# Scores two blocks ahead, staged softmax and even conversion in the first 23 blocks of an attention and feed-forward kernel

## The chip, the cores and the metric

One core of a Trainium2 chip runs the whole program. The metric is the device time of one execution in microseconds (us); the median of several executions is quoted. A ratio is the mean time of one kernel's fast runs over the mean of the other's fast runs of the same rounds, so it isn't quite the ratio of the medians beside it; its bracket is a 95% interval. Ratios are to the kernel before, which ran again beside each group of experiments (medians 1627.9 to 1629.3).

Engines: PE multiplies matrices, DVE, ACT and POOL work on vectors, SP issues most transfers. Each has its own queue.

## The reference

Attention over 8 batches of 8 heads, 576 tokens of 64 elements, keeps only scores within tau of the row's maximum. Its output, 4608 x 512, goes through a feed-forward layer with a squared relu. The two weight matrices are float64, so the kernel has to convert them.

```python
scores = scale * np.matmul(q, k.transpose(0, 1, 3, 2))          # 1/8 * q k^T
thresh = np.max(scores, axis=-1, keepdims=True) - tau
scores = np.where(scores >= thresh, scores, -1000000000.0)
attn = np.exp(scores - max)                                     # cut: max of the row
attn = attn / (np.sum(attn, axis=-1, keepdims=True) + 1e-09)
x = np.matmul(attn, v)                                          # reshaped to 4608 x 512
h = np.maximum(x @ w_in, 0.0)                                   # w_in 512 x 2048
return (h * h @ w_out).astype(np.float32)                       # w_out 2048 x 512
```

## The kernel before

A *block* is 128 query rows of two heads. The first 23 blocks run while the weights arrive and are converted, one chunk of 128 x 512 a *step*. A chunk passes three stages:

```python
def convert1(m):
    a = conv.tile([P, WC], FP32, tag="a", bufs=2, name="a")
    nc.scalar.activation(out=a, in_=hi, func=AF.Abs)                  # ACT  "a"
    nc.gpsimd.tensor_scalar(out=a, in0=a, ... op0=ALU.min, op1=ALU.max)  # POOL clamp
    r = conv.tile([P, WC], I32, tag="r", bufs=2, name="r")            # two buffers
    nc.scalar.activation(out=r, in_=lo, func=AF.Copy, scale=2.0**-29) # ACT  "r"
def convert2(m):      # two DVE operations on the raw words (shift, merge)
def convert3(m):      # POOL: w_in or w_out = raw + r; frees r
    nc.gpsimd.tensor_tensor(out=chunks[m][0], in0=lo, in1=r, op=ALU.add)

def weights_step():   # (cut)
    m = at_step["n"]; at_step["n"] = m + 1
    convert3(m - 4)
    convert1(m - 2)   # its r is the buffer that convert3(m - 4) reads
    convert2(m - 3)
    if m < len(chunks): fetch(m)
```

With two buffers, the new `r` of a step may be written only after the POOL addition of the same step. In the old softmax a step stands between the exponentials (ACT) and the masks (DVE), so POOL gets that addition ahead of the block's normalisation:

```python
def begin(n, between=lambda: None):
    i, t = slots[n]
    job = softmax(i, t, scores(i, t))
    next(job)            # maxima, threshold, exponentials
    between()            # weights_step()
    next(job, None)      # masks with row sums, +1e-9, reciprocal, POOL normalisation
```

Of the kernel before, what the change touches and what calls it, by code (L numbers as in the profile page):

```python
# [13 lines left out]
ALU = mybir.AluOpType  # L14
# [5 lines left out]
def kernel(  # L20
# [27 lines left out]
    nc = tc.nc  # L48
    B, H, S, D = q.shape
    P = 128  # L50
    DM, FF = moe_w_in.shape
# [114 lines left out]
    def minus(e, out, x, y):  # L166
        e.tensor_tensor(out=out, in0=x, in1=y, op=ALU.subtract)  # L167

    def plus(e, out, x, y):
        e.tensor_tensor(out=out, in0=x, in1=y, op=ALU.add)  # L170

    def combine_in(n):

        e = nc.gpsimd
        first, second = ts(n, WC), ds(HF + n * WC, WC)
        a11, a12 = w_in[:, 0:2, first], w_in[:, 2:4, first]
        a21, a22 = w_in[:, 0:2, second], w_in[:, 2:4, second]
        s1, s2, s4 = (s_in[:, m, :, first] for m in range(3))
        yield plus(e, s1, a21, a22)
        yield minus(e, a21, a11, a21)  # L180
        yield minus(e, s2, s1, a11)
        yield minus(e, s4, a12, s2)

    def combine_out(k):

        first, second = ds(k, 4), ds(KF + k, 4)
        b11, b12 = w_out[:, first, 0:HD], w_out[:, first, HD:DM]
        b21, b22 = w_out[:, second, 0:HD], w_out[:, second, HD:DM]
        t1, t2, t4 = (t_out[0][:, m, first, :] for m in range(3))
        minus(nc.vector, t1, b12, b11)  # L190
        yield minus(nc.gpsimd, b12, b22, b12)
        minus(nc.vector, t2, b22, t1)
        yield minus(nc.gpsimd, t4, b21, t2)

    w_out_t = moe_w_out.rearrange("(f p) o -> p f o", p=P)
    chunks = [
# [8 lines left out]
    def weights_step():  # L205

        m = at_step["n"]
        at_step["n"] = m + 1
        convert3(m - 4)
        convert1(m - 2)  # L210
        convert2(m - 3)
        if m < len(chunks):
            fetch(m)
        if m - 4 in (n_in // 2 - 1, n_in - 1):
            sums_due.append(combine_in((m - 4) // (n_in // 2)))
        if m == len(chunks) + 3:
            early.close()
            late = ctx.enter_context(tc.tile_pool(name="late", bufs=1, side="right"))
            t_out.append(late.tile([P, 3, KF, HD], FP32, name="t_out"))
            sums_due.extend(combine_out(k) for k in range(0, KF, 4))  # L220

    def sums_step():
        while sums_due:
# [55 lines left out]
    def turn(i):  # L279
        qn, kn, rn = loaded.pop(i)  # L280
        qT = sb.tile([P, S], FP32, tag="qT", bufs=2, name="qT")
        kT = sb.tile([P, S], FP32, tag="kT", bufs=2, name="kT")
        _, t0, t1 = visits[i]
        for nat, to, u0, u1 in ((qn, qT, t0, min(t1, FULL)), (kn, kT, 0, FULL)):
            pt = bank([P, FULL, P], "pqk")
            for t in range(u0, u1):
                nc.tensor.transpose(pt[:, t, :], nat[:, t, :], ident[:, :])  # L287
            flat, to = pt[:, u0:u1, :].rearrange("p t m -> p (t m)"), to[:, u0 * P : u1 * P]
            if nat is qn:
                nc.scalar.activation(out=to, in_=flat, func=AF.Identity, scale=qscale[:, :])  # L290
            else:
                nc.vector.tensor_copy(out=to, in_=flat)
        pt = bank([P, P], "pqkr")
        nc.tensor.transpose(pt[:, :], rn[:, :], ident[:, :])
        nc.scalar.activation(out=qT[:, MAIN:S], in_=pt[:, 0:REST], func=AF.Identity, scale=qscale[:, :])
        nc.scalar.copy(kT[:, MAIN:S], pt[:, REST:P])
        if i < NP:
            for j in range(2):
                rows = ds(j * D, D)
                nc.gpsimd.tensor_copy(out=kdiag[i % 2][rows, ds(j * REST, REST)], in_=kT[rows, MAIN:S])  # L300
        turned[i] = (qT, kT)
# [31 lines left out]
    def softmax(i, t, sc):  # L333

        nj = 2 if t < FULL else 1
        at = (0, (psum["n"] - 1) * BANK - REST)[0:nj]
        sm = sb.tile([P, 2], FP32, tag="sm", bufs=3, name="sm")
        nmx = sb.tile([P, 2], FP32, tag="nmx", bufs=3, name="nmx")
        for j in range(nj):
            nc.vector.tensor_reduce(  # L340
                out=nmx[:, j : j + 1], in_=sc[:, ds(at[j], S)], axis=AXIS.X, op=ALU.max, negate=True
            )

        thr = sb.tile([P, 2], FP32, tag="thr", bufs=3, name="thr")
        nc.vector.tensor_scalar(
            out=thr[:, 0:nj], in0=nmx[:, 0:nj], scalar1=-1.0, scalar2=tau_p[:, :], op0=ALU.mult, op1=ALU.subtract
        )
        w = sb.tile([P, 2 * S], FP32, tag="w", bufs=2, name="w")
        for j in range(nj):
            nc.scalar.activation(  # L350
                out=w[:, ts(j, S)], in_=sc[:, ds(at[j], S)], func=AF.Exp, bias=nmx[:, j : j + 1], scale=1.0
            )
        yield
        for j in range(nj):
            nc.vector.scalar_tensor_tensor(  # L355
                out=w[:, ts(j, S)], in0=sc[:, ds(at[j], S)], scalar=thr[:, j : j + 1], in1=w[:, ts(j, S)],
                op0=ALU.is_ge, op1=ALU.mult, accum_out=sm[:, j : j + 1],
            )
        nc.vector.tensor_scalar(out=sm[:, 0:nj], in0=sm[:, 0:nj], scalar1=1e-9, scalar2=None, op0=ALU.add)
        nc.vector.reciprocal(out=sm[:, 0:nj], in_=sm[:, 0:nj])  # L360
        if t == FULL:

            normalize(w[:, S : S + REST], w[:, MAIN:S], sm[:, 0:1])
        for j in range(nj):
            normalize(w[:, ts(j, S)], w[:, ts(j, S)], sm[:, j : j + 1])
        weights[i, t] = w
# [257 lines left out]
    slots = [(i, t) for i, (_, t0, t1) in enumerate(visits) for t in range(t0, t1)]  # L624
    n_first, n_batch = NP * HALF, NP * NB

    def begin(n, between=lambda: None):
        i, t = slots[n]
        job = softmax(i, t, scores(i, t))
        next(job)  # L630
        between()
        next(job, None)

    def values_after(n):

# [9 lines left out]
            feed_forward_until(b * S + min(t1 * P, S))  # L645
        return True

    def turns(n):

        i, t = slots[n]  # L650
        return i + 1 < len(visits) and t == max(visits[i][2] - 2, visits[i][1])

    def slot(n, steps):


        def weights_due(k):
            if k < steps:
                if at_step["n"] < N_STEPS:
                    weights_step()
                sums_step()  # L660

        if turns(n):
            turn(slots[n][0] + 1)
        if n + 1 < len(slots):
            begin(n + 1, lambda: weights_due(0))
        with_values = values_after(n - 1)
        if turns(n) and slots[n][0] + 2 < len(visits):
            load(slots[n][0] + 2)
        i, t = slots[n - 1]
        if with_values and part_of(t)[1] == visits[i][2] and i + 2 < len(visits):  # L670
            load_v(i + 2)
        transposes(*slots[n])
        for k in range(1, steps):
            weights_due(k)
        return with_values

    ET = mybir.EngineType
    with ExitStack() as stack, tc.manual_schedule(engines={ET.PE, ET.DVE, ET.Activation, ET.Pool}):
        open_psum(stack, 3, 2, 2)
        load(0)  # L680
        for _ in range(2):
            weights_step()
        load(1)
        load_v(0)
        load_v(1)
        turn(0)
        begin(0)
        for n in range(n_first - 1):
            slot(n, 1)
    with ExitStack() as stack:  # L690
        g_pool = stack.enter_context(tc.tile_pool(name="g", bufs=1))
        open_psum(stack, 4, 1, 4)
        late = 0.0

        n_early = n_first - 1 + (N_STEPS + 4 - n_first) // 2
        for n in range(n_first - 1, len(slots)):
            early_on = n < n_early
            with tc.manual_schedule(engines={ET.PE, ET.DVE, ET.Activation, ET.Pool} if early_on else {ET.PE}):
                with_values = slot(n, 2 if early_on else 1)
                if n < n_first:  # L700
                    continue


                if early_on:
                    per_slot = 14 * U_IN / (n_early - n_first)
                elif n < n_batch:
                    per_slot = (asked["us"] + PIECE) / (2 * n_batch - n)
                elif n < 2 * n_batch:
                    per_slot = asked["us"] / (2 * n_batch - n)
                else:  # L710
                    per_slot = asked["us"] / (n_batch - n % n_batch)

                late = min(run(per_slot * (0.7 if with_values else 1.2) + late), 0.0)
        with tc.manual_schedule(engines={ET.PE}):
            values_after(len(slots) - 1)
            run(float("inf"))


def as_float(bits):
# [33 lines left out]
```

## Time and profile before

| kernel before | |
|---|---|
| time, median of 3 (range) | 1628.0 us (1627.81 to 1628.55) |
| profiled span, mean granted PE clock | 1626.5 us, 0.971 |
| the cut: transposes of block 23 done | 231.6 us |
| after the cut | 1394.9 us, PE busy 97% |
| ACT waiting for POOL before r, up to the cut | 44.9 us |

The cut splits the span into a stretch that the change rewrites, bound by a chain of waits, and one bound by PE. The lines stand in the prediction below. A line of the waits reads: engine, its instruction, "<-" what ended the wait, then the sum in us, how often, and the longest.

### The profile page before, as it was taken

Reading aid. Unit: us, or ns where it says so; the run is one execution under the profiler, and the core shown is the slowest. Engines: PE = TensorE matmul, PEld = TensorE weight load, DVE = VectorE, ACT = ScalarE, POOL = GpSimd, SP = SyncE. Lnnn points to the kernel's source line nnn. Section 1 sums busy time; section 2 is a strip of 40 time slices with the busy share of each in tenths; the row PEclk is TensorE's granted clock in tenths of the full one; section 3 lists DMA queues with packets and bytes.
Section 4 is the critical chain, followed back from the end, with each engine's and each line's share of the span. In section 5 each row is a group of like instructions: output and inputs, shape, how many; then the busy total and the mean of one; then the engine's idle time right before and its main releaser. Section 6 shows DMA issues by size and latency. Waiting matters only on the chain.

```text
span 1626.5 us, 25919 instructions
## 1 busy us (share of the span) xinstructions
PE 1515.6 (93%) x10084; PEld 1216.1 (75%) x10084; DVE 867.0 (53%) x1792; ACT 585.7 (36%) x1273; POOL 592.1 (36%) x630
## 2 busy tenths in 40 slices
PE   5676789999999999999999999999999999999998
PEld 2344567778787778778788887878777787878987
DVE  4678974645555564646444455555646464553222
ACT  3545633434343333433333243333433333431100
POOL 2488662332424232334141424232423333233131
PEclk8877889999999999999999999999999999999999
DMA  4334401111010101010101010101011101000000
GB/s 126 109 108 131 128 22 35 23 29 30 23 36 14 31 23 35 23 36 16 35 8 30 21 36 10 34 23 35 23 36 23 35 16 29 15 1 14 14 14 14
DMA packets 107914, 58.69 MB, mean 36 GB/s; under 512 B 89873, under 2 KB 99089, under 8 KB 107793
## 3 DMA queue, kind: packets, MB, share of 16 engines
q1 hardware_dynamic: 107792, 57.04, 12.9%
q8 instruction: 80, 1.31, 0.3%
q14 instruction: 42, 0.34, 0.1%
HBM read 47.58 MB, written 9.44 MB: 35 GB/s over the span
## 4 chain that ended last, share of the span: by engine, by line
PE 77%; DVE 12%; ACT 6%; POOL 3%; issue 2%; SPq 0%; DMA 0%; ACTq 0%; DVEq 0%; POOLq 0%
PE ph L482 27%; PE po L556 25%; PE sc L326 11%; PE pwT L397 6%; DVE nmx L340 5%; ACT w L350 4%; PE pv L428 3%; PE pqk L287 2%; PE pwR L386 2%; DVE s L170 1%; DVE w L355 1%; ACT x L436 1%; PE pv L423 1%; DVE g L491 1%; POOL w L369 1%
## 5 line engine op out<-in xcount | busy, mean ns | idle before, releaser
L369 POOL TENSOR_SCALAR w<-w,sm 128x576 f32<-128x576 f32 (+1 forms) x320 | 237.4, 752 | 643.9 <-DVE sm L360 638.4
L340 DVE TENSOR_REDUCE nmx<-sc 128x1 f32<-128x576 f32 x288 | 206.1, 752 | 206.7 <-PE sc L326 188.9
L355 DVE SCALAR_TENSOR_TENSOR w<-sc,thr,w 128x576 f32<-128x576 f32 x288 | 225.0, 815 | 132.7 <-ACT w L350 130.2
L350 ACT ACTIVATE w<-sc,nmx 128x576 f32<-128x576 f32 x288 | 199.8, 741 | 259.0 <-DVE nmx L340 258.9
L556 PE MATMUL po<-w_out,g 128*128 128x256 f32 x1152 | 261.5, 382 | 11.2 <-ACT x L436 6.1
L556 PEld LDWEIGHTS po<-w_out,g 128*128 128x128 f32 x1152 | 216.1, 191 | 41.0 <-ACT x L436 7.3
L326 PE MATMUL sc<-kT,qT 64*128 64x64 f32 (+3 forms) x1248 | 215.6, 461 | 24.5 <-DVE w L355 24.4
L482 PE MATMUL ph<-x,w_in 128*128 128x128 f32 x1728 | 209.5, 278 | 2.1 <-ACT x L436 2.1
L326 PEld LDWEIGHTS sc<-kT,qT 64*128 64x128 f32 (+1 forms) x1248 | 105.5, 181 | 137.1 <-issue 124.6
L482 PEld LDWEIGHTS ph<-x,w_in 128*128 128x128 f32 x1728 | 203.2, 195 | 3.2 <-ACT x L436 2.3
L397 PE MATMUL pwT<-ident,w 128*128 128x128 f32 x1024 | 146.3, 281 | 44.2 <-ACT x L436 25.7
L397 PEld LDWEIGHTS pwT<-ident,w 128*128 128x128 f32 x1024 | 117.1, 143 | 56.8 <-ACT x L436 37.1
L398 ACT COPY wT<-pwT 128x512 f32<-128x512 f32 x256 | 145.2, 594 | 24.6 <-PE pwT L397 20.8
L482 PE MATMUL ph<-xt,s_in 128*128 128x128 f32 x1152 | 142.4, 278 | 4.3 <-POOL s_in L167 3.3
L428 PE MATMUL pv<-wT,va 128*64 128x320 f32 (+1 forms) x1024 | 141.8, 420 | 0.0
L482 PEld LDWEIGHTS ph<-xt,s_in 128*128 128x128 f32 x1152 | 136.0, 194 | 6.2 <-POOL s_in L167 4.9
L170 DVE TENSOR_TENSOR u<-ph,u 128x512 f32<-128x512 f32 x108 | 74.6, 690 | 112.4 <-PE ph L482 84.2
L556 PE MATMUL po<-t_out,g 128*128 128x256 f32 x576 | 132.2, 379 | 0.0
L428 PEld LDWEIGHTS pv<-wT,va 128*64 128x64 f32 x1024 | 69.4, 140 | 66.5 <-issue 29.9
L556 PEld LDWEIGHTS po<-t_out,g 128*128 128x128 f32 x576 | 107.7, 190 | 13.5
L493 POOL TENSOR_TENSOR g<-p 128x512 f32<-128x512 f32 x36 | 37.8, 1049 | 156.4 <-ACT p L510 156.4
L482 PE MATMUL ph<-x,s_in 128*128 128x128 f32 x576 | 71.9, 279 | 0.0
(79 smaller groups left out, 1623.6 us busy)
## 6 DMA issues: line engine op xcount, KB each, us to landing
kn<-in_k_dram SPq DMA_DIRECT2D x72, 128.0 KB, 3.1
va<-in_v_dram SPq DMA_DIRECT2D x36, 256.0 KB, 2.8
out_dram<-o SPq DMA_DIRECT2D x36, 256.0 KB, 2.0
raw<-in_moe_w_in_dram SPq DMA_DIRECT2D x16, 512.0 KB, 4.0
raw<-in_moe_w_out_dram SPq DMA_DIRECT2D x16, 512.0 KB, 3.8
qn<-in_q_dram SPq DMA_DIRECT2D x56, 128.0 KB, 2.4
rn<-in_q_dram SPq DMA_DIRECT2D x36, 32.0 KB, 2.4
rn<-in_k_dram SPq DMA_DIRECT2D x36, 32.0 KB, 2.7
```

Of the source, the lines that this page charges most:

```text
L170: e.tensor_tensor(out=out, in0=x, in1=y, op=ALU.add)
L326: nc.tensor.matmul(to, qT[rows, ds(t * P, m)], kT[rows, ds(k0, n)], start=True, stop=True)
L340: nc.vector.tensor_reduce(out=nmx[:, j : j + 1], in_=sc[:, ds(at[j], S)], axis=AXIS.X, op=ALU.max, negate=True)
L350: nc.scalar.activation(out=w[:, ts(j, S)], in_=sc[:, ds(at[j], S)], func=AF.Exp, bias=nmx[:, j : j + 1], scale=1.0)
L355: nc.vector.scalar_tensor_tensor(out=w[:, ts(j, S)], in0=sc[:, ds(at[j], S)], scalar=thr[:, j : j + 1], in1=w[:, ts(j, S)], op0=ALU.is_ge, ...
L369: nc.gpsimd.tensor_scalar(out=out, in0=w, scalar1=r, scalar2=1.0, op0=ALU.mult, op1=ALU.mult)
L397: nc.tensor.transpose(pt[:, c, :], w[:, ds(j * (S + REST) + c * P, P)], ident[:, :])
L398: nc.scalar.copy(wT[:, j, :, at], pt[:, :, :])
L428: nc.tensor.matmul(pv[rows, :], va[:, j, c, :], wT[:, j, c, 0:n], start=False, stop=(c == FULL - 1), skip_group_check=True,)
L482: nc.tensor.matmul(to[:, j, :], a, b, start=(not more and j == 0 and c == 0), stop=(c == 1), skip_group_check=True,)
L493: e.tensor_tensor(out=to, in0=c[:, :, :], in1=c[:, :, :], op=ALU.mult)
L556: nc.tensor.matmul(to[:, :], a[:, f, :], b[:, f, :], start=(not more and f == 0), stop=(f == KF - 1), skip_group_check=True,)
```

## The change

Its intent: take scores and maxima out of the chain of a block by computing them two blocks ahead in two three-bank buffers, and let the stages of two succeeding softmaxes interleave. With it come even conversion (two steps on even blocks, one on odd), two tiny operations moved from DVE to POOL, the first feed-forward products grouped by bank, and the output weights' sums regrouped. The core of the diff:

```diff
 def softmax(i, t, sc):
+        early = psum["n"] == 3
+        small = nc.gpsimd if early else nc.vector
 ...
+            if early and j == 0:
+                yield                      # after the first maximum
-        nc.vector.tensor_scalar(           # threshold
+        small.tensor_scalar(
 ...
+        if early:
+            yield                          # before the exponentials
 ...
-        nc.vector.tensor_scalar(out=sm ... scalar1=1e-9 ...)
+        small.tensor_scalar(out=sm ... scalar1=1e-9 ...)
+        if early:
+            yield
         nc.vector.reciprocal(...)          # then the POOL normalisation
 ...
+    def early_slot(n, last, steps, ff_steps):
+        if n < last:
+            ahead(n + 2)                   # scores, two blocks ahead
+        stage(n + 1)                       # exponentials, masks, 1e-9
+        stage(n + 2)                       # first maximum
+        stage(n + 1)                       # reciprocal, POOL normalisation
+        if n < last:
+            turn_until(n + 3)
+        stage(n + 2)                       # second maximum, threshold
+        if steps:
+            weights_step()
+        for _ in range(ff_steps):
+            run(0.1)
+        values_and_load(n)
+        transposes(*slots[n])
+        for _ in range(steps - 1):
+            weights_step()
+        sums_step()
 ...
+        FF_STEPS = {11: 3, 12: 4, 17: 3, 18: 4}
+            steps = min(2 - n % 2, N_STEPS - at_step["n"])
```

The normalisation is now issued before `weights_step()`, so POOL's addition, and with it ACT's `r`, stands behind it.

More of the change, by code (lines that the diff above doesn't have):

```diff
@@ L179, in combine_in, with combine_out @@
         yield plus(e, s1, a21, a22)
+        yield minus(e, s2, s1, a11)
         yield minus(e, a21, a11, a21)
-        yield minus(e, s2, s1, a11)
         yield minus(e, s4, a12, s2)
-    def combine_out(k):
-        first, second = ds(k, 4), ds(KF + k, 4)
-        b11, b12 = w_out[:, first, 0:HD], w_out[:, first, HD:DM]
-        b21, b22 = w_out[:, second, 0:HD], w_out[:, second, HD:DM]
-        t1, t2, t4 = (t_out[0][:, m, first, :] for m in range(3))
-        minus(nc.vector, t1, b12, b11)
-        yield minus(nc.gpsimd, b12, b22, b12)
-        minus(nc.vector, t2, b22, t1)
-        yield minus(nc.gpsimd, t4, b21, t2)
+    def combine_out():
+        for what in range(2):
+            for k in range(0, KF, 4):
+                first, second = ds(k, 4), ds(KF + k, 4)
+                b11, b12 = w_out[:, first, 0:HD], w_out[:, first, HD:DM]
+                b21, b22 = w_out[:, second, 0:HD], w_out[:, second, HD:DM]
+                t1, t2, t4 = (t_out[0][:, m, first, :] for m in range(3))
+                if what == 0:
+                    minus(nc.vector, t1, b12, b11)
+                    yield minus(nc.gpsimd, b12, b22, b12)
+                else:
+                    minus(nc.vector, t2, b22, t1)
+                    yield minus(nc.gpsimd, t4, b21, t2)
     w_out_t = moe_w_out.rearrange("(f p) o -> p f o", p=P)
@@ L219, in weights_step @@
             t_out.append(late.tile([P, 3, KF, HD], FP32, name="t_out"))
-            sums_due.extend(combine_out(k) for k in range(0, KF, 4))
+            sums_due.append(combine_out())
     def sums_step():
@@ L296, in turn @@
         nc.scalar.copy(kT[:, MAIN:S], pt[:, REST:P])
-        if i < NP:
+        if psum["n"] == 3:
             for j in range(2):
@@ L352, in softmax @@
             )
-        yield
         for j in range(nj):
@@ L358, in softmax @@
             )
-        nc.vector.tensor_scalar(out=sm[:, 0:nj], in0=sm[:, 0:nj], scalar1=1e-9, scalar2=None, op0=ALU.add)
+        small.tensor_scalar(out=sm[:, 0:nj], in0=sm[:, 0:nj], scalar1=1e-9, scalar2=None, op0=ALU.add)
+        if early:
+            yield
         nc.vector.reciprocal(out=sm[:, 0:nj], in_=sm[:, 0:nj])
@@ L625, with begin @@
     n_first, n_batch = NP * HALF, NP * NB
-    def begin(n, between=lambda: None):
+    def begin(n):
         i, t = slots[n]
-        job = softmax(i, t, scores(i, t))
-        next(job)
-        between()
-        next(job, None)
+        for _ in softmax(i, t, scores(i, t)):
+            pass
     def values_after(n):
@@ L646, in values_after, with turn_until, values_and_load @@
         return True
-    def turns(n):
-        i, t = slots[n]
-        return i + 1 < len(visits) and t == max(visits[i][2] - 2, visits[i][1])
-    def slot(n, steps):
-        def weights_due(k):
-            if k < steps:
-                if at_step["n"] < N_STEPS:
-                    weights_step()
-                sums_step()
-        if turns(n):
-            turn(slots[n][0] + 1)
-        if n + 1 < len(slots):
-            begin(n + 1, lambda: weights_due(0))
+    first_slot = [n for n, (i, t) in enumerate(slots) if t == visits[i][1]]
+    turned_to = {"n": 0}
+    def turn_until(n):
+        i = turned_to["n"]
+        if i == len(visits) or first_slot[i] > n:
+            return
+        turn(i)
+        turned_to["n"] = i + 1
+        if i + 1 < len(visits):
+            load(i + 1)
+    def values_and_load(n):
         with_values = values_after(n - 1)
-        if turns(n) and slots[n][0] + 2 < len(visits):
-            load(slots[n][0] + 2)
         i, t = slots[n - 1]
@@ L671, in slot, with stage, ahead @@
             load_v(i + 2)
+        return with_values
+    def slot(n):
+        turn_until(n + 2)
+        if n + 1 < len(slots):
+            begin(n + 1)
+        with_values = values_and_load(n)
         transposes(*slots[n])
-        for k in range(1, steps):
-            weights_due(k)
-        return with_values
+        return with_values
+    jobs = {}
+    def stage(n):
+        if n in jobs:
+            next(jobs[n], None)
+    def ahead(n):
+        i, t = slots[n]
+        jobs[n] = softmax(i, t, scores(i, t))
+    def early_slot(n, last, steps, ff_steps):
[16 more added lines that the diff above has]
+        sums_step()
     ET = mybir.EngineType
-    with ExitStack() as stack, tc.manual_schedule(engines={ET.PE, ET.DVE, ET.Activation, ET.Pool}):
+    ALL = {ET.PE, ET.DVE, ET.Activation, ET.Pool}
+    g_pool = ctx.enter_context(tc.tile_pool(name="g", bufs=1))
+    with ExitStack() as stack, tc.manual_schedule(engines=ALL):
         open_psum(stack, 3, 2, 2)
@@ L682 @@
             weights_step()
-        load(1)
         load_v(0)
+        turn_until(0)
+        ahead(0)
+        stage(0), stage(0)
         load_v(1)
-        turn(0)
-        begin(0)
-        for n in range(n_first - 1):
-            slot(n, 1)
-    with ExitStack() as stack:
-        g_pool = stack.enter_context(tc.tile_pool(name="g", bufs=1))
+        ahead(1)
+        stage(0), stage(1), stage(0), stage(1)
+        turn_until(2)
+        FF_STEPS = {11: 3, 12: 4, 17: 3, 18: 4}
+        n = 0
+        while at_step["n"] < N_STEPS:
+            steps = min(2 - n % 2, N_STEPS - at_step["n"])
+            early_slot(n, 10**6, steps, FF_STEPS.get(n, 0))
+            n += 1
+        early_slot(n, n, 0, 0)
+        while sums_due:
+            sums_step()
+        n_early = n + 1
+    with ExitStack() as stack, tc.manual_schedule(engines={ET.PE}):
         open_psum(stack, 4, 1, 4)
         late = 0.0
-        n_early = n_first - 1 + (N_STEPS + 4 - n_first) // 2
-        for n in range(n_first - 1, len(slots)):
-            early_on = n < n_early
-            with tc.manual_schedule(engines={ET.PE, ET.DVE, ET.Activation, ET.Pool} if early_on else {ET.PE}):
-                with_values = slot(n, 2 if early_on else 1)
-                if n < n_first:
-                    continue
-                if early_on:
-                    per_slot = 14 * U_IN / (n_early - n_first)
-                elif n < n_batch:
-                    per_slot = (asked["us"] + PIECE) / (2 * n_batch - n)
-                elif n < 2 * n_batch:
-                    per_slot = asked["us"] / (2 * n_batch - n)
-                else:
-                    per_slot = asked["us"] / (n_batch - n % n_batch)
-                late = min(run(per_slot * (0.7 if with_values else 1.2) + late), 0.0)
-        with tc.manual_schedule(engines={ET.PE}):
-            values_after(len(slots) - 1)
-            run(float("inf"))
+        for n in range(n_early, len(slots)):
+            with_values = slot(n)
+            if n < 2 * n_batch:
+                per_slot = asked["us"] / (2 * n_batch - n)
+            else:
+                per_slot = asked["us"] / (n_batch - n % n_batch)
+            late = min(run(per_slot * (0.7 if with_values else 1.2) + late), 0.0)
+        values_after(len(slots) - 1)
+        run(float("inf"))
 def as_float(bits):
```

## The prediction

> **What bounds the kernel now.** I read the page's slices first, then three stretches side by side, then the waits of the first stretch, then that stretch in order of time. The slices say where idle TensorE time is left:
>
> ```profile
> PE   5676789999999999999999999999999999999998
> PEclk8877889999999999999999999999999999999999
> ```
>
> One slice is 40.7 us. Only the first six have PE below 90% and a clock below full. The cut at 232 us is where both kernels stand at the same place of their PE program: the transposes of block 23 are done, the 14 product groups of the first feed-forward piece are done, and the first output product comes next (the PE order of both builds shows this, and the trace has the first "po" at 231.6 us).
>
> ```profile
> core 0: us, PE busy (x) PEld busy (x) DVE busy (x) ACT busy (x) POOL busy (x), PEclk, DMA share, GB/s
> 0.00:75.00 75.00, 46.37 (x200) 25.51 (x200) 38.34 (x91) 32.57 (x69) 25.27 (x45) 0.82 0.44 120
> 75.00:232.00 157.00, 112.12 (x648) 79.80 (x647) 131.53 (x210) 79.24 (x169) 124.89 (x111) 0.80 0.37 104
> 232.00:1626.00 1394.00, 1357.11 (x9239) 1110.78 (x9238) 697.09 (x1492) 473.94 (x1037) 441.94 (x474) 1.00 0.09 24
> ```
>
> After 232 us PE is busy 1357 of 1394 us (97%) at full clock: that part is bound by PE, its work is the same in the changed kernel, and I carry it over unchanged. Before it no engine is full (DVE 170 of 232 us, POOL 150, ACT 112), so a chain of waits bounds it: 24 blocks in 231.6 us. Who waits there:
>
> ```profile
> ACT w L350 <- DVE nmx L340: 47.6, 16, 8.6
> ...
> ACT r L144 <- POOL w_out L164: 24.7, 9, 5.7
> POOL w L369 <- DVE sm L360: 21.9, 18, 6.7
> ACT r L144 <- POOL w_in L164: 20.2, 6, 5.6
> ```
>
> The exponential waits for the maximum of scores just computed, and the conversion's second activation (r) waits 45 us in all for POOL's last conversion step. The reader should keep that second wait in mind. One early block in order of time:
>
> ```profile
> 42.49 0.49 PE L330 MATMUL sc<-kdiag,qT 128*128 128x128 f32 x2
> ...
> 43.02 1.42 DVE L340 TENSOR_REDUCE nmx<-sc 128x1 f32<-128x576 f32 x2 [2.02 <-PE sc L330]
> ...
> 44.53 1.37 ACT L350 ACTIVATE w<-sc,nmx 128x576 f32<-128x576 f32 x2 [2.30 <-DVE nmx L340]
> ...
> 45.94 0.82 DVE L355 SCALAR_TENSOR_TENSOR w<-sc,thr,w 128x576 f32<-128x576 f32 x1 [0.18 <-ACT w L350]
> 46.35 0.66 ACT L144 ACTIVATE r<-raw 128x512 int32<-128x512 uint32 x1
> ...
> 46.91 0.25 ACT L388 COPY wR<-pwR 128x128 f32<-128x128 f32 x1
> ...
> 47.21 1.12 PE L397 MATMUL pwT<-ident,w 128*128 128x128 f32 x4 [3.69 <-ACT wR L388]
> ...
> 47.54 0.17 DVE L359 TENSOR_SCALAR sm<-sm 128x2 f32<-128x2 f32 x1
> 47.74 0.17 DVE L360 RECIPROCAL sm<-sm 128x2 f32<-128x2 f32 x1
> ...
> 48.07 1.47 POOL L369 TENSOR_SCALAR w<-w,sm 128x576 f32<-128x576 f32 x2 [0.92 <-DVE sm L360]
> 48.37 0.58 ACT L398 COPY wT<-pwT 128x512 f32<-128x512 f32 x1 [0.72 <-PE pwT L397]
> ```
>
> Read it as a loop: scores, maxima 1.42, exponentials 1.37, the activations a and r (1.1 from start to start), copy of the remainder, the last four transposes 1.12, and only then the next scores, because PE runs in order. Scores of succeeding blocks start at 41.4, 50.3, 58.2, 67.0 and 75.1 us: 8.4 us a block with one conversion each. From 76 to 231 us, with two conversions a block, the single four-bank buffer and the feed-forward, it is about 9.7.
>
> **What the Trainium skill says.** "PSUM — Partial Sum Buffer", Engine vs sequencer instructions: ScalarE, VectorE and GpSimdE queues are strict FIFO. The trace agrees: the copy at 46.91 starts only after r at 46.35, though its transpose had been done since 43. My argument rests on this. "SBUF — State Buffer", Who interferes with whom: DVE in a two-port mode, or with two SBUF inputs, and GpSimd exclude each other for a whole instruction. The trace agrees: the DVE conversion shift takes 0.42 us alone but 906 ns on average over the first 232 us. "TensorE: Matmul & The Clock Gate", What's actually happening: idle windows of about 3.4 us halve PE's clock; the first four transposes of that block take 0.60 us, the last four, after 3.7 us of waiting, 1.12.
>
> **The change, part by part.**
>
> *Removed from the loop:* the scores and the wait for the fresh maximum. Scores now come two blocks ahead in two three-bank buffers, and the maxima of block n+2 are taken while block n+1 is finished. Alone, this takes some 4 us (scores 2.5, maxima 1.4) off the loop.
>
> *Moved:* the threshold and the 1e-9 addition go from DVE to POOL. DVE loses at most 10.0+8.2 us over the stretch, much of it lock waiting; POOL gains two tiny operations a block, about 0.2 us each (an estimate from the 0.23 us of the small kdiag copies).
>
> *Even conversion:* two steps on even blocks and one on odd, from the start, 34 in 23 blocks; the same total work.
>
> *Added:* here the build's order and its semaphore waits decide. In a block POOL now has: 1e-9, two normalisations (n+1), the threshold (n+2), and only then the conversion's last step. ACT has: exponentials (n+1), a, r, the copies of block n, on even blocks another a and r, exponentials (n+2). r uses one of two buffers, and waits for the POOL conversion step of the same turn. So this closed loop is in the program, one block long: exponentials (n+1), DVE masks, DVE maximum (n+2), reciprocal, POOL normalisations, threshold, conversion, ACT r, copies, exponentials (n+2). With durations of the block above:
>
> - exponentials and hand-over 1.41; masks 1.60 (45.94 to 47.54); one maximum 0.71; reciprocal and hand-over 0.33: 4.05
> - normalisations 1.47, plus 0.25 which I choose for the DVE conversion now colliding with the second one; threshold 0.25: 1.97
> - POOL conversion 1.29, hand-over 0.04, r to the copy 0.56: 1.89
> - copy to transposes 0.30, transposes and hand-over 1.16 (cold clock), copy 0.48: 1.94
>
> Sum 9.85 us on an odd block. An even block adds a and r, 1.12: 11.0. A turn adds the two kdiag copies, 0.5, and a block with values 0.2.
>
> Blocks 1 to 20 have an r: ten at 9.85 and ten at 11.0, turns 7 x 0.5, values 8 x 0.2, less about 2 for each of four half-size blocks: 205 us. *Feed-forward:* with two banks, grouped products put PE work into that loop in blocks 11, 12, 17 and 18. In 11 and 17 the value product waits for the bank which the relu frees: copy 0.7, second product group 2.2, relu 0.7, values 3.1, some 6.7 us. In 12 and 18 the five DVE additions stand before the transposes' banks, some 3.4. Together 20. The start up to the reciprocal of block 2 I walk through as 27 us, and blocks 21 to 23, without r, take 5 and 3.
>
> 27 + 205 + 20 + 8 = 260 us against 231.6: about 29 longer. The regrouped output sums leave POOL two 2.35 us operations just after the cut; I charge 2 us. 1628 + 31 gives 1659, and I put 1660.
>
> **Rivals.**
>
> *The overlap works.* If POOL's late conversion step did not stop ACT, the bound would be the fullest engine: POOL's 150 us plus 10, or DVE's 170 less what the moves free. With start-up that is 175 to 190 us for the stretch, 40 to 55 us less, a time near 1580. For it speaks that no engine is full before and that scores, maxima and exponentials wait so long. Against it: the wait of r on POOL costs 45 us already in the old order, where that step stands ahead of the normalisation, and the build shows it behind. Even with no cold clock (0.5 less), no collision (0.25) and half the feed-forward cost, 20 blocks bring the cut to about 235, not below 230.
>
> *Idle moves but little changes.* If normalisations overlap better and PE stays warm, the loop is near 9.1 and 10.2, the cut near 240, the time 1635 to 1645.
>
> *More is lost.* A longer ACT wait leaves PE idle over 3 us a block, so its clock drops; at half clock the grouped products, 2 us each, take 3 to 4, and collisions of DVE with POOL's 2.35 us sums fall into the loop. Then the cut is at 275 to 285, and the time 1670 to 1685.
>
> **Range and chances.** The closed loop is in the program, so I give gain over 2% (below 1596) only 6%, for the case that I misread an order. The centre is almost on the upper edge of the 2% band (1660.6): 0.46 within and 0.48 slower. The 8-in-10 range, 1636 to 1685, spans the last two rivals.
>
> **What would show it.** In the changed profile: the first output product near 260 us and the rest still about 1395 us; r waiting for POOL's w_in and w_out steps rising from 45 us to 70 or more, with 3 to 4 us each time; the wait of exponentials for maxima nearly gone; the early clock no higher than 0.8; alternating block periods of about 10 and 11 us, and blocks 11 and 17 near 17. I am wrong if the blocks come every 7 us, or if r hardly waits: then the POOL order did not bind. I am also wrong if the stretch after the cut changes by over 10 us.

## The result, and the profile after

The changed kernel takes **1679.82 us** (1676.79 to 1680.05, 4 runs) against 1627.9 (1627.66 to 1628.55). The ratio is 1.0314 [1.0296, 1.0332]: 3.1% slower. That is inside the predicted range, 20 us above the predicted time. Its profiled span is 1678.1 us.

The slices of the page of the changed kernel, 42 us each:

```profile
PE   5557477999999999999999999999999999999999
PEclk8777777999999999999999999999999999999999
```

At the start, seven slices instead of six are now below 90%, and they are emptier. The three stretches, with the cut at 276 us:

```profile
core 0: us, PE busy (x) PEld busy (x) DVE busy (x) ACT busy (x) POOL busy (x), PEclk, DMA share, GB/s
0.00:75.00 75.00, 40.44 (x166) 21.85 (x167) 36.51 (x72) 31.39 (x64) 31.06 (x59) 0.83 0.45 121
75.00:276.00 201.00, 126.78 (x657) 81.67 (x658) 105.61 (x179) 82.13 (x174) 129.23 (x156) 0.76 0.29 81
276.00:1678.00 1402.00, 1362.36 (x9240) 1112.70 (x9240) 707.05 (x1492) 473.81 (x1036) 454.26 (x479) 0.99 0.09 24
```

More exactly the cut lies at 275.8 us, where it was 231.6: 44.2 us of the 51.6 us more of span. The other 7.4 come after it (1402.3 against 1394.9). No engine is full: DVE is busy for 142 of the first 276 us, POOL for 160. What ACT waits for up to the cut:

```profile
ACT r L144 <- POOL w_in L164: 58.8, 11, 6.5
ACT r L144 <- POOL w_out L164: 48.3, 9, 7.0
...
ACT w L360 <- DVE nmx L346: 7.2, 3, 3.8
```

The exponentials' wait for maxima has fallen from 47.6 to 7.2 us, as the change intends. The wait of `r` for POOL has risen from 44.9 to 107.1 us, 20 times. One even block in order of time (start, duration, then engine, line and operation; the bracket is idle time before it and what ended it):

```profile
57.57 1.38 ACT L360 ACTIVATE w<-sc,nmx 128x576 f32<-128x576 f32 x2
...
59.44 0.82 DVE L364 SCALAR_TENSOR_TENSOR w<-sc,thr,w 128x576 f32<-128x576 f32 x1 [6.18 <-PE sc L330]
...
61.59 0.16 DVE L371 RECIPROCAL sm<-sm 128x2 f32<-128x2 f32 x1
...
62.27 2.14 POOL L380 TENSOR_SCALAR w<-w,sm 128x576 f32<-128x576 f32 x2 [0.96 <-DVE sm L371]
...
64.41 0.31 POOL L353 TENSOR_SCALAR thr<-nmx,tau_p 128x2 f32<-128x2 f32 x1
64.68 1.28 POOL L164 TENSOR_TENSOR w_in<-raw,r 128x512 int32<-128x512 int32 x1
...
66.00 0.67 ACT L144 ACTIVATE r<-raw 128x512 int32<-128x512 uint32 x1 [6.51 <-POOL w_in L164]
...
66.82 0.27 ACT L399 COPY wR<-pwR 128x128 f32<-128x128 f32 x1
...
66.98 1.82 PE L408 MATMUL pwT<-ident,w 128*128 128x128 f32 x8 [4.29 <-ACT x L447]
...
69.88 0.66 ACT L144 ACTIVATE r<-raw 128x512 int32<-128x512 uint32 x1
...
70.43 1.37 ACT L360 ACTIVATE w<-sc,nmx 128x576 f32<-128x576 f32 x2
```

Follow the starts: exponentials, masks, reciprocal, normalisation, threshold, POOL's addition, `r`, the copy, the transposes, a second `r`, and the next exponentials 12.86 us after the first. (Three of its parts are longer than in other blocks; the sum below sets two of those beside it.) ACT stands still 6.51 us before `r`, and PE 4.29 us behind ACT, because the copies that free PE's banks stand behind `r`. The scores two blocks ahead are long ready; nobody can use them.

After the cut, the start of the tail shows where part of the 7.4 us goes:

```profile
277.01 1.21 DVE L167 TENSOR_TENSOR t_out<-w_out 128x1024 f32<-128x1024 f32 x1
277.26 3.88 POOL L380 TENSOR_SCALAR w<-w,sm 128x64 f32<-128x64 f32 x2 [0.36 <-PE sc L330]
...
281.19 0.47 PE L397 MATMUL pwR<-ident,w 128*128 128x128 f32 x1 [4.06 <-POOL w L380]
```

The regrouped weight sums run on DVE beside POOL's normalisation of block 24 (one operation of 128 x 64 and one of 128 x 576), which takes 3.88 us where it took 1.15 in the kernel before, and PE waits 4.06 us for it. Only then, at 282.3 us, comes the first output product.

### The profile page after: what moved, and what is told of

Read it like the earlier page. It is cut to its first block, busy times and chain, and to the rows that moved or that the text cites. A ratio compares the mean times of both kernels' runs of the same rounds, so it can differ in the third digit from the quotient of the medians.

```text
span 1678.1 us, 25857 instructions
## 1 busy us (share of the span) xinstructions
PE 1529.6 (91%) x10060; PEld 1216.2 (72%) x10060; DVE 849.2 (51%) x1742; ACT 587.3 (35%) x1273; POOL 614.5 (37%) x692
## 3 DMA queue, kind: packets, MB, share of 16 engines
q8 instruction: 80, 1.31, 0.3%
## 4 chain that ended last, share of the span: by engine, by line
PE 75%; DVE 10%; ACT 7%; POOL 5%; issue 2%; DMA 0%; SPq 0%; ACTq 0%; DVEq 0%; POOLq 0%
PE ph L493 27%; PE po L567 24%; PE sc L330 10%; PE pwT L408 6%; DVE nmx L346 4%; ACT w L360 4%; PE pv L439 3%; DVE w L364 2%; POOL w L380 2%; PE pwR L397 2%; PE pqk L291 1%; DVE s L170 1%; ACT x L447 1%; PE pv L434 1%; DVE g L167 1%
## 5 line engine op out<-in xcount | busy, mean ns | idle before, releaser
L567 PE MATMUL po<-w_out,g 128*128 128x256 f32 x1152 | 265.9, 385 | 7.7 <-DVE g L167 7.1
L408 PE MATMUL pwT<-ident,w 128*128 128x128 f32 x1024 | 152.5, 287 | 80.7 <-ACT x L447 40.3
L330 PE MATMUL sc<-kT,qT 64*128 64x512 f32 (+3 forms) x1200 | 214.4, 474 | 11.8 <-DVE w L364 8.7
L330 PEld LDWEIGHTS sc<-kT,qT 64*128 64x128 f32 (+1 forms) x1200 | 99.1, 181 | 120.4 <-issue 98.5
L439 PEld LDWEIGHTS pv<-wT,va 128*64 128x64 f32 x1024 | 69.3, 139 | 65.9 <-issue 27.8
L493 PE MATMUL ph<-xt,w_in 128*128 128x128 f32 x576 | 70.4, 275 | 1.4 <-DVE u L170 1.4
```

Of the source, the lines that this page charges most:

```text
L330: nc.tensor.matmul(to, qT[rows, ds(t * P, m)], kT[rows, ds(k0, n)], start=True, stop=True)
L408: nc.tensor.transpose(pt[:, c, :], w[:, ds(j * (S + REST) + c * P, P)], ident[:, :])
L439: nc.tensor.matmul(pv[rows, :], va[:, j, c, :], wT[:, j, c, 0:n], start=False, stop=(c == FULL - 1), skip_group_check=True,)
L493: nc.tensor.matmul(to[:, j, :], a, b, start=(not more and j == 0 and c == 0), stop=(c == 1), skip_group_check=True,)
L567: nc.tensor.matmul(to[:, :], a[:, f, :], b[:, f, :], start=(not more and f == 0), stop=(f == KF - 1), skip_group_check=True,)
```

## The experiments

**Theory 1:** the loss comes from `r` waiting for a POOL addition that now stands behind the normalisation. **Rivals:** the small operations on POOL; the grouped feed-forward products; the even conversion; or a full or colliding pair of POOL and DVE, whatever the order. All kernels gave correct results. The cut is read as in the profiles above, and "after cut" is the profiled span less the cut.

| run | time, median | ratio to before | cut | after cut |
|---|---|---|---|---|
| before | 1627.9 | 1 | 231.6 | 1394.9 |
| after | 1679.8 | 1.0314 | 275.8 | 1402.3 |
| r3 | 1633.2 | 1.0027 | 231.2 | 1398.9 |
| conv_first | 1635.1 | 1.0042 | 231.6 | 1400.5 |
| before_r3 | 1627.0 | 0.9994 | 229.1 | 1396.1 |
| small_dve | 1675.8 | 1.0292 | 274.4 | 1400.6 |
| ff_late | 1679.5 | 1.0304 | 252.8 | 1425.4 |
| r3_ff_late | 1630.4 | 1.0004 | 201.7 | 1426.8 |
| r3_clamp | 1641.2 | 1.0071 | 234.5 | 1403.0 |
| r3_clamp_xt | 1638.1 | 1.0050 | 237.1 | 1399.1 |
| r3_free | 1626.0 | 0.9980 | 223.7 | 1402.7 |
| before_even | 1621.7 | 0.9960 | 223.7 | 1395.6 |
| r3_free_dve | 1616.4 | 0.9919 | 215.6 | 1397.7 |
| before_late3 | 1686.9 | 1.0353 | 290.9 | 1393.9 |

### r3: a third buffer for r in the changed kernel

```diff
-        r = conv.tile([P, WC], I32, tag="r", bufs=2, name="r")
+        r = conv.tile([P, WC], I32, tag="r", bufs=3, name="r")
```

> The changed kernel with three r buffers in place of two, nothing else. Theory 1 (r waits for POOL's last conversion step behind the normalisations, and holds up ACT's copies and the next exponentials): r's wait for POOL falls from 107 us to under 50, the loop shrinks to about 8 us a block (on even blocks the second r still waits for the first step), the cut after the transposes of block 23 moves from 276 us to about 215, the time is 1610 to 1630. Theory 2 (a full engine or the DVE-POOL handing to and fro of threshold and 1e-9 bounds the block): the cut stays above 260 us, the time 1665 to 1682.

Measured: 1633.16 us (1628.62 to 1635.01), ratio 1.0027 [1.0007, 1.0047]. The cut moves by 44.6 us, and the time by 46.7 of the 52 us lost. Nothing is removed from any engine. The waits of `r` for POOL up to 232 us in this run:

```profile
ACT r L144 <- POOL w_out L164: 5.0, 5, 1.5
...
ACT r L144 <- POOL w_in L164: 4.4, 5, 1.9
```

107.1 us have become 9.4 (the two sums). The third buffer lets `r` wait for the addition of the step before instead of that of its own step. The direction is theory 1's, but I had hoped for more: the time lies 3 us above my range and the cut 16 us after my 215.

### conv_first: the order instead of the buffer

```diff
         if n < last:
             ahead(n + 2)
+        convert3(at_step["n"] - 4)
         stage(n + 1)
```

> The changed kernel with two r buffers, but the first conversion step of a block is issued on POOL ahead of the 1e-9 addition and the normalisations. Theory 1: same cause removed by order in place of a buffer, so r's first wait goes; on even blocks the second r still waits behind the normalisations, a loop of about 8 us; cut at 210 to 230 us, time 1610 to 1635. Theory 2: POOL's work is the same, cut above 260, time 1665 to 1682.

Measured: 1635.09 us, ratio 1.0042 [1.0027, 1.0056]. With two buffers still, but with POOL's addition ahead of the normalisation, the cut comes at 231.6. A different edit to the same wait has the same result, so it isn't memory or an accident of placement that made r3 faster. Here `r` still waits 36.0 us for POOL up to the cut (19.4 and 16.6), 26.6 us more than in r3, and yet the cut is the same within 0.5 us: the sum of a wait is not its price.

### before_r3: the third buffer in the kernel before

The edit of r3, in the kernel before.

> The kernel before with three r buffers: the control. Theory 1: its early blocks are bound by scores, maxima, exponentials, so the first 75 us stay; between 75 and 232 us r waits some, so 0 to 12 us less: 1616 to 1628. If a third r buffer alone gave as much here as in the changed kernel (over 40 us), the r wait would not be what the change brought in.

Measured: 1627.02 us, ratio 0.9994 [0.9979, 1.0009], cut 2.5 us earlier. The control shows that a third buffer is worth nothing clear of noise by itself. It isn't that `r` had nothing to wait for. Up to the cut of this run:

```profile
ACT w L350 <- DVE nmx L340: 76.7, 25, 10.8
...
ACT r L144 <- POOL w_in L164: 1.0, 1, 1.0
```

With 0.4 us for w_out, `r` waits 1.4 us instead of 44.9, but the exponentials wait 76.7 us for their maxima instead of 47.6. In the old order the wait of `r` cost next to nothing, because the wait for the maxima took its place.

### small_dve: threshold and 1e-9 back on DVE

```diff
-        small = nc.gpsimd if early else nc.vector
+        small = nc.vector
```

> The changed kernel with threshold and 1e-9 back on DVE. Theory 1: the threshold leaves POOL's queue ahead of the conversion step (0.3 us a block less in the loop), the 1e-9 comes back behind DVE work: within 10 us, 1668 to 1688. Theory 2 (the handing to and fro over POOL bounds the block): 30 us or more faster, under 1650.

Measured: 1675.79 us, ratio 1.0292 [1.0277, 1.0308]; this interval overlaps that of the changed kernel. The cut moves by 1.4 us. `r` still waits 100.2 us for POOL (55.8 and 44.4). The tiny operations aren't the cause.

### ff_late and r3_ff_late: no feed-forward product before the cut

```diff
-        FF_STEPS = {11: 3, 12: 4, 17: 3, 18: 4}
+        FF_STEPS = {}
```

> The changed kernel with no feed-forward products among the first 23 blocks: the 14 product groups of the first piece go to the blocks after. My prediction's term: they put 20 us into the early loop, so the cut (end of the transposes of block 23) moves from 276 to 250 to 258 us, and 14 groups of 1.8 us (25 us of PE) come after it: time within 8 us of the changed kernel, 1672 to 1686. If the cut moves by under 10 us the term was too large; by over 30 too small, and the time drops below 1672.

> The same on the version with three r buffers. There blocks 11, 12, 17, 18 took some 36 us more than their neighbours, so the cut should move from 231 to about 195 and the time from 1633 to 1618 to 1626. If the products were hidden beside other waits, the time rises by up to 25 us to 1658.

Measured: ff_late 1679.47 us (1.0304), cut 23.0 us earlier; r3_ff_late 1630.43 us (1.0004 [0.9989, 1.0019]), cut 29.5 us earlier than in r3. In both the time after the cut grows by as much (23.1 and 27.9 us). The time of r3_ff_late and its cut are 4 and 7 us above what I expected. So the grouped products cost the early stretch about what my sum said, 23.0 us for 20 in the changed kernel, but the same PE work costs that much wherever it lies; grouping them early neither loses nor gains.

### r3_clamp and r3_clamp_xt: half of the conversion moved

r3 with, in each block,

```diff
         stage(n + 1)
+        if steps:
+            convert1(at_step["n"] - 2)    # a, clamp, r ahead of the first maximum of n + 2
         stage(n + 2)
```

and in r3_clamp_xt also the four sums of the first feed-forward input after block 9 instead of at block 11 (`if n == 9: combine_x(0)`).

> Three r buffers, and a and r with POOL's clamp issued ahead of the normalisations. In the r3 trace DVE's second conversion of even blocks waits 23 us in all for that clamp, so even blocks are near 9.3 us and odd ones 6.5. If this is what is left of the loop, even blocks fall to about 7.5, the cut from 231 to about 212, the time to 1608 to 1620. If POOL itself is full by then, no change: 1628 to 1638.

> The same with the sums of the first piece's x made on POOL after block 9, in place of block 11, where PE waited 5.4 us for them: 4 to 8 us less than r3_clamp, if the products' place in the loop is what costs there; no change if those sums only move the wait.

Measured: r3_clamp 1641.22 us (1.0071 [1.0056, 1.0086]), a clear miss: I had expected a gain over r3 and it lost 8 us. r3_clamp_xt, at 1638.07 us, is 3 us better than r3_clamp, where I had expected 4 to 8; its cut is even later (237.1 against 234.5), so what it gains lies after the cut. In r3_clamp the starts of the remainder's transposes still came 10.5 and 11.2 us apart on even blocks and 7.0 on odd ones. The second `r` of an even block still waited for a POOL addition that stood behind the normalisation (1.71 us for the one at 57.15): I had moved one wait out of the loop and left its twin in. That can explain why nothing was gained; why 8 us were lost stays open.

### r3_free: both moved

```diff
+        if steps:
+            convert3(at_step["n"] - 4)
         stage(n + 1)
+        if steps:
+            convert1(at_step["n"] - 2)
         stage(n + 2)
```

> The changed kernel with three r buffers, and in each block the POOL conversion step moved ahead of the first softmax stage and the pair a, r of the next chunk with it between the stages, so that no activation of the conversion and no DVE shift stands behind a normalisation of the same block. Theory A (in the three-buffer version the even blocks are set by conversion steps that still queue behind the normalisation and the threshold; the earlier attempt moved only half of them): even blocks fall from about 9.3 to about 7.5 us, the cut (transposes of block 23) comes at 205 to 215 us instead of 231, and the time is 1605 to 1622. Theory B (with the r wait gone the stretch is bound by POOL and DVE work that excludes each other and by the landing of the raw chunks, whatever the order): the cut stays at 226 to 238 us and the time at 1628 to 1642.

Measured: 1625.97 us (1623.26 to 1628.18), ratio 0.9980 [0.9963, 0.9996]; cut 223.7 us. Each theory was half right. The two-head blocks of the first visits now come every 7.0 to 7.2 us, even and odd alike (remainder transposes at 43.81, 50.87, 58.08 and 65.05 us), which is theory A; the kernel before takes 8.4. But the cut fell between the two predictions, because the next visits are bound by something else. The next block has its transposes at 67.99 and the one after at 83.09 us. POOL in between, with the DVE operation that waits for it:

```profile
70.41 2.36 POOL L170 TENSOR_TENSOR s_in<-w_in 128x1024 f32<-128x1024 f32 x1
...
72.72 1.29 POOL L164 TENSOR_TENSOR w_in<-raw,r 128x512 int32<-128x512 int32 x1
...
74.11 0.22 POOL L368 TENSOR_SCALAR sm<-sm 128x2 f32<-128x2 f32 x1
74.36 0.17 DVE L371 RECIPROCAL sm<-sm 128x2 f32<-128x2 f32 x1 [2.19 <-POOL sm L368]
...
75.11 2.16 POOL L380 TENSOR_SCALAR w<-w,sm 128x576 f32<-128x576 f32 x2
```

The 0.22 us addition of 1e-9 stands behind a weight sum of 2.36 and a conversion step of 1.29 us. DVE idles 2.19 us for it, and the normalisation and the next exponentials follow late. With `r` freed, the placement of the small operations should begin to matter.

### r3_free_dve: and the small operations back on DVE

r3_free with the edit of small_dve.

> The version with three r buffers and the reordered conversion, with the threshold and the 1e-9 addition back on DVE. In that version's trace DVE waits 16.8 us for the 1e-9 addition on POOL, which stands behind the 2.35 us weight sums and the last conversion step. Theory (with r freed, POOL sets the pace of the three-block visits): cut 213 to 220 us instead of 223.7, time 1615 to 1623. Rival (DVE, which would take on the two small operations and their lock waits, sets it): cut 223 or later, time 1625 to 1632.

Measured: 1616.36 us (1615.04 to 1617.83), ratio 0.9919 [0.9899, 0.9938]; cut 215.6 us. Both numbers lie in the range of the theory, outside that of the rival. The same edit brought 4 us in the changed kernel, with overlapping intervals, and 9.6 us here. This version beats both kernels: 3.8% below the changed one and 0.8% below the kernel before (medians), which is clear of the noise but small. Its slices:

```profile
PE   6775889999999999999999999999999999999998
...
PEclk9879899999999999999999999999999999999999
```

### before_even: the even conversion alone, in the kernel before

```diff
-            slot(n, 1)
+            slot(n, 2 - n % 2)
 ...
-        n_early = n_first - 1 + (N_STEPS + 4 - n_first) // 2
+        n_early = 23
 ...
-                with_values = slot(n, 2 if early_on else 1)
+                with_values = slot(n, (2 - n % 2) if early_on else 1)
```

> The kernel before with one part of the change alone: two conversion steps on every even block and one on every odd one from the start, in place of one a block at first and two a block later. Theory A (the loss of the change comes from r standing behind the normalisation, which this order of the softmax does not have): the time stays within 1620 to 1640 and the r wait for POOL under 60 us. Rival (the even conversion itself costs the early blocks, because it puts second activations into blocks that had one): cut at 245 us or later, time 1643 to 1660.

Measured: 1621.69 us, ratio 0.9960 [0.9945, 0.9975]; cut 223.7 us, `r` waits 25.3 us. So this part of the change is a small gain, and not the cause of the loss.

### before_late3: the suspected order put into the kernel before

```diff
         next(job)
-        between()
         next(job, None)
+        between()
```

> The mirror: the kernel before with one thing of the change put into it, the whole conversion step placed after the normalisation instead of between the exponentials and the masks. If r waiting behind the normalisation is the cause, the loop scores, maxima, exponentials, masks, normalisation, last conversion step, r, copy, transposes, scores closes at about 10.3 us in the blocks of one step instead of 8.4, and some 1.5 us more in the blocks of two: the cut goes from 231.6 to 255 to 275, the waits of r for POOL from 45 us to over 80, the time to 1650 to 1675. Rival (the loss belongs to the scores-ahead order, and the place of the conversion does not matter by itself): cut below 240, time 1622 to 1638.

Measured: 1686.89 us (1686.47 to 1690.04), ratio 1.0353 [1.0334, 1.0372]; cut 290.9 us. No scores ahead, no even conversion, no small operations on POOL, and yet the loss is as large as the whole change's, indeed larger than I expected. One block of this run:

```profile
51.63 1.37 ACT L350 ACTIVATE w<-sc,nmx 128x576 f32<-128x576 f32 x2 [3.47 <-DVE nmx L340]
...
54.84 0.17 DVE L360 RECIPROCAL sm<-sm 128x2 f32<-128x2 f32 x1
...
55.18 1.93 POOL L369 TENSOR_SCALAR w<-w,sm 128x576 f32<-128x576 f32 x2 [9.92 <-DVE sm L360]
...
57.08 1.28 POOL L164 TENSOR_TENSOR w_in<-raw,r 128x512 int32<-128x512 int32 x1
58.39 0.67 ACT L144 ACTIVATE r<-raw 128x512 int32<-128x512 uint32 x1 [4.84 <-POOL w_in L164]
...
58.96 0.25 ACT L388 COPY wR<-pwR 128x128 f32<-128x128 f32 x1
...
59.26 1.12 PE L397 MATMUL pwT<-ident,w 128*128 128x128 f32 x4 [8.64 <-ACT wR L388]
```

It is the chain of the changed kernel: normalisation, addition, `r`, copy, transposes, with PE idle 8.64 us at its end. `r` waits 95.1 us for POOL up to the cut (57.4 and 37.7). The additions of succeeding blocks start at 43.27 and 57.08 us, so this loop takes 13.8 us, not 10.3. Part of the excess is seen: after so much idle time PE is slow (its granted clock is 0.79 over the first 75 us and 0.74 from there to the cut, against 0.82 and 0.80 in the kernel before), and the scores that stand in this loop take 2.08 + 0.60 us where the block shown in the prediction's section takes 1.13 + 0.49, so that the maxima start 1.1 us later; the normalisations take 1.93 us instead of 1.47. The rest was not broken down. One limit: this edit moves the whole step, so DVE's conversion operations and the clamp move with the addition; together with r3 and conv_first, which touch `r` and the addition alone, that isn't a gap in the argument.

## Why the prediction was right, and where its sizes were off

**The mechanism: right, and shown.** The closed loop of one block, through the normalisation, POOL's addition and `r`, sets the early stretch. Cutting it by a buffer (r3) or by order (conv_first) takes back 45 to 47 of 52 us; adding it to the kernel before (before_late3) costs 58. The predicted signs are there: `r` waits 107.1 us where I said 70 or more, 5.4 us each time rather than 3 to 4; the exponentials' wait is nearly gone; blocks alternate, 12.6, 10.6, 12.8, 10.7 and 12.9 us between remainder transposes. The clock is 0.83 and then 0.76, where I had said no higher than 0.8, so the first 75 us miss that by a little.

One of its supports was misread. I argued that the wait of `r` costs 45 us already in the old order. The wait is there, but before_r3 takes it away and gains nothing: off the longest chain, it had no price. In the changed kernel the same wait stands in the closed loop, and there it has one. And the verdict was close to a toss: the direction was argued, but I gave 0.48 to a loss over 2% and 0.46 to less, with the centre 20 us too low. (A slip without weight: of the slices before, the last is below 90% too.)

**The rivals.** "The overlap works" was worth more in my words than on the chip. I gave it a stretch of 175 to 190 us once `r` didn't bind. With `r` free the cut is 231.2 us (r3). Moving the conversion ahead of the normalisation brings it to 223.7 (r3_free), and taking the small operations off POOL to 215.6 (r3_free_dve): other queues on POOL take the place of the wait. "More is lost" came true in its numbers: cut at 275 to 285, time 1670 to 1685. Of its reasons the slow clock is seen (eight transposes took 1.82 us in the block shown, 1.09 in a block of r3_free), the products cost 23 us for 20, and collisions with the 2.35 us sums were not measured apart.

**The terms of the sum.** Three blocks against my sum, in us, between starts: the even block shown above, the even block whose exponentials start at 34.76, and the odd one at 70.43. My 11.2 for an even block includes 0.2 for the values; an odd block with a turn (the change to the next heads' queries and keys, with two kdiag copies) is 9.85 + 0.5.

| part of the loop | predicted | even, 57.57 | even, 34.76 | odd, 70.43 |
|---|---|---|---|---|
| exponentials to masks | 1.41 | 1.87 | 1.47 | 1.40 |
| masks and one maximum, to the reciprocal | 2.31 | 2.15 | 2.15 | 2.15 |
| reciprocal to normalisation | 0.33 | 0.68 | 0.32 | 0.33 |
| normalisation pair | 1.72 | 2.14 | 1.63 | 1.41 |
| kdiag copies after a turn | 0.5 | none | none | 1.27 |
| threshold | 0.25 | 0.27 | 0.69 | 0.28 |
| POOL addition to r | 1.33 | 1.32 | 1.31 | 1.32 |
| r to the remainder's copy (with the values' copy) | 0.56 (0.76) | 0.82 | 0.83 | 0.57 |
| copies and transposes, to the next a or exponentials | 1.94 | 2.50 | 2.64 | 1.93 |
| a and r | 1.12, even | 1.11 | 1.11 | none |
| block | 11.2; odd 10.35 | 12.86 | 12.15 | 10.66 |

POOL ahead of its addition, in the odd block and then in the even one at 34.76:

```profile
74.31 1.47 POOL L380 TENSOR_SCALAR w<-w,sm 128x576 f32<-128x576 f32 x2 [0.61 <-DVE sm L371]
...
75.72 1.16 POOL L304 COPY kdiag<-kT 64x64 f32<-64x64 f32 x2
...
76.99 0.31 POOL L353 TENSOR_SCALAR thr<-nmx,tau_p 128x2 f32<-128x2 f32 x1
77.27 1.29 POOL L164 TENSOR_TENSOR w_in<-raw,r 128x512 int32<-128x512 int32 x1
```

```profile
40.33 0.72 POOL L353 TENSOR_SCALAR thr<-nmx,tau_p 128x2 f32<-128x2 f32 x1
41.02 1.28 POOL L164 TENSOR_TENSOR w_in<-raw,r 128x512 int32<-128x512 int32 x1
```

Three terms were too small in the usual block: the threshold (0.69 for 0.25 in the block at 34.76; its median over the stretch is 0.72 us, against my estimate of 0.2), the copies after a turn (1.27 for 0.5), and the slow transposes of even blocks (0.56 and 0.70 more). The 1e-9 was right (0.22). The block shown adds something of its own: its hand-overs ahead of the masks and of the normalisation (0.46 and 0.35 over) and its normalisations (2.14) exceed those of the nine other blocks up to block 9, which have 1.40 to 1.79, 0.25 to 0.33 and 1.46 to 1.63. There the 0.25 us that I chose for a collision with DVE's conversion was even a little too much.

For the stretch as a whole:

| term | predicted | measured |
|---|---|---|
| start, to the reciprocal of block 2 | 27 | 27.8 |
| blocks 1 to 20 without feed-forward | 205 | 213 |
| feed-forward in it | 20 | 23 (ff_late) |
| blocks 21 to 23, to the cut | 8 | 11.6 |
| cut | 260 | 275.8 |
| after the cut | 1397 | 1402.3 |

The 213 is what is left of 236.4 us, from that reciprocal to the one of block 22, after the 23. "Blocks 11 and 17 near 17" was a miss: 27.1 and 22.6 us between transposes. The products' sum was about right. Their places were not: block 11 takes 11.2 us more than without them and block 17 takes 6.4, where I had 6.7 for each. Above all the blocks under them were longer than my 10 or so: without any products they still take 15.9 and 16.2 us (ff_late).

**After the cut** I had charged 2 us and it is 7.4. The trace shows one wait of 4.06 us behind POOL there. I had also said that the first output product follows the cut at once; in the changed order the scores of block 25 and the transposes of block 24 come first, and this wait lies in front of them. All versions with the new order pay 3 to 8 us there, unless the products themselves were moved behind the cut. How much of it the regrouped weight sums cause was not tested apart and stays open.

**Where the expected gain went.** Even without the wait of `r`, the scores ahead only equal the kernel before (r3). The blocks that they speed up, 8.4 to about 7.1 us in r3_free, are paid back later. Part of it is shown: the small operations behind POOL's sums and conversion in a three-block visit (9.6 us, r3_free_dve). The rest, in those visits and after the cut, was not taken apart.

## What to carry to other kernels

When stages are interleaved, list for every buffer who frees it and what stands ahead of the freeing instruction in its engine's queue: here a POOL addition that moved behind a normalisation made ACT wait, and through ACT everything. If such a wait closes a loop, one more buffer or an earlier place of one instruction cuts it, and a mirror test in the old kernel proves it. Don't take the size of a wait for its price: `r` waited 44.9 us in the kernel before and removing that gained nothing, while removing 97.7 of the 107.1 us in the changed kernel gained 46.7. Move all its twins at once, and look again at what you had found harmless: the small operations cost 4 us, hardly clear of the noise, while the wait hid them, and 9.6 us when it was gone.

## What the Trainium skill lacked or had wrong

- "Trainium Kernel Development and Optimization", Best Practices, advises double-buffering to overlap transfers with compute. It says nothing on how many buffers two compute engines need between them: here two against three buffers for `r` made 46.7 us in the changed kernel (1679.82 against 1633.16) and nothing clear of noise in the kernel before (ratio 0.9994).
- "SBUF — State Buffer", Who interferes with whom, gives the rule of the lock but no sizes for short POOL operations. The threshold on POOL (128 x 2) took 0.31 to 0.73 us with a median of 0.72; the pair of normalisations of a full block 1.47 us in the block shown in the prediction and 2.14 beside DVE's conversion; that of block 24 (128 x 64 and 128 x 576) 1.15 us in the kernel before and 3.88 beside DVE subtractions with two inputs.
- "TensorE: Matmul & The Clock Gate", HAM oscillation — how this bites in real kernels, has its worked example of a PE that turns slow in every turn of a loop behind waits for DMA. It has none behind a chain of ACT and POOL. Here PE's waits for ACT's copies, 2.7 to 7.3 us in most early blocks, went with a mean granted clock of 0.76 over 201 us, and eight transposes took 1.82 us in the block shown, where 1.09 us was seen in the faster r3_free.
